# Reading the keys' columns in six orders in the products that find the score maxima

## The chip, the cores and the metric

The kernel runs on one core of one Trainium2 chip. The metric is the device time of one execution in microseconds (us). Before the change it is 1575.32 us, the median of two runs (1575.31 and 1575.34).

## The reference

Attention with 32 heads that share one head of keys and values, a gated feed-forward block (GLU), and a gate that mixes the two. All tensors are float32; S is 2048, D is 512, a head is 16 wide, F is 1792.

```python
q = (x @ wq).reshape(B, S, H, Dh).transpose(0, 2, 1, 3)
k, v = x @ wk, x @ wv                                   # one head for all
p = softmax(einsum("bhqd,bkd->bhqk", q, k) * Dh ** -0.5)
a = einsum("bhqk,bkd->bhqd", p, v) ... @ wo
b = (sigmoid(x @ w_gate) * (x @ w_up)) @ w_down
g = sigmoid((x * gate_w).sum(-1, keepdims=True))
return g * a + (1 - g) * b
```

## The kernel before, in words

The kernel makes the softmax in two passes. A **unit** is a block of 512 queries and a group of four heads; there are 32 units (4 blocks by 8 groups). For each unit the first pass makes all scores with queries on the partitions and keys along the columns, and takes the maximum of each row (`maximum`, 64 products and 64 reductions a unit, 2048 in all). The second pass makes the scores again, the other way round (`scores`, keys on the partitions), with the maximum subtracted inside the product, and ScalarE takes the exponential. The third step multiplies the exponentials with the values (`pv`).

The keys stand in SBUF in one tile `ks`, 128 partitions by 2048 columns of float32. Rows 0 to 63 and rows 64 to 127 hold copies, so that two products of 64 rows each can run beside each other on the two halves of TensorE's array. `HALF[h]` picks the half. In `maximum`, the weights (first operand) are 128 queries of one head, `qs_t[u % 3][r, pr, part(qt)]`, and the moving operand is 512 neighbouring columns of `ks`; the result is a whole PSUM bank of 128x512, from which VectorE's `tensor_reduce` takes one maximum per partition. The operands of these products, of `scores` and of the feed-forward products (`fill`) are of the type float32r; the profile prints them as f32. Of the large groups only `pv` has operands of plain float32: each of its products stands in the trace as two matmuls, 4096 for 2048, in groups of four that use four bands of 32 columns of the array together.

What runs when is fixed in the program. A long string `ORDER` names the steps, and `State.step` turns each character into instructions; nothing is decided at run time but waits on semaphores. A hex digit is one **slot**: one product for the upper half and one for the lower, decoded by `divmod(int(code, 16), 4)`, where 1 is a maximum, 2 a score and 3 a feed-forward product. So `5` is a slot with a maximum in both halves, `7` and `d` one with a maximum and a feed-forward product, `6` and `9` one with a maximum and a score. `V` is one step of `pv`, which uses the whole array. TensorE takes its products in this order; the lists of VectorE, ScalarE, GpSimd and the DMA queue follow from it. The eight banks of PSUM are shared by all.

Of the kernel before, what the change touches and what calls it, by code (L numbers as in the profile page):

```python
# [725 lines left out]
def tile_kernel(ctx, tc, x_in, wq, wkv, wo, wg, wu, wd, consts_in, out):  # L726
    nc = tc.nc
# [13 lines left out]
    banks = [pp.tile([P, 512], F32, tag=f"bank{i}", name=f"bank{i}") for i in range(8)]  # L741
# [13 lines left out]
    def split(raw, hl, hi, lo):  # L755
        hi(hl[:, 0, :], raw)
        lo.tensor_tensor(hl[:, 1, :], raw, f32(hl[:, 0, :]), op=ALU.subtract)  # L757
        return hl
# [81 lines left out]
    part = lambda i: slice(i * P, (i + 1) * P)  # L840
# [30 lines left out]
    qs_t = [cp.tile([P, 2, TB], F32R, name=f"qs{i}") for i in range(3)]  # L871
# [22 lines left out]
    ks = cp.tile([P, S], F32R, name="ks")  # L894
# [238 lines left out]
    def h_split(_, b, f):  # L1133
        hl = fp.tile([P, 2, TB], F32R, tag="hl", name=f"hl{b}_{f}", bufs=HB)
        HS[b, f] = split(HS[b, f], hl, nc.gpsimd.tensor_copy, nc.gpsimd)

    def maximum(h, n, i):
        s, pr = divmod(n, 2)
        u, n = divmod(s, NC)
        qt, kb = divmod(n, 4) if u else (n % 4, n // 4)  # L1140
        r = HALF[h]
        nc.tensor.matmul(banks[i], qs_t[u % 3][r, pr, part(qt)], ks[r, kb * 512:(kb + 1) * 512],  # L1142
                         start=True, stop=True)
        nc.vector.tensor_reduce(MX[u][:, pr, h, qt, kb:kb + 1], banks[i], axis=AX.X, op=ALU.max)  # L1144

    def scores(h, n, i):
# [13 lines left out]
        "load": load_item, "w_hi": w_hi, "w": w_split, "x_hi": x_hi, "x": x_lo,  # L1160
        "f": fill, "gate": gate, "gated": gated, "h": h_split, "part": part_of, "add": add_part, "out": send_out,
        "m": maximum, "max_finish": max_finish, "max_split": max_split, "max_square": max_square,
        "send_max": send_max, "place_max": place_max, "s": scores,
        "values": on_bank(pv), "finish": on_bank(finish), "store": store, "sums": sums, "invert": invert, "send_inverse": send_inverse,
# [28 lines left out]
    for i in range(2):  # L1193
        for j in range(4):
            for t in (2 * i, 2 * i + 1):
                r, m = HALF[t % 2], slice(32 * j, 32 * j + 32)
# [63 lines left out]
```

## Time and profile before

| | |
|---|---|
| time, two runs | 1575.34 and 1575.31 us |
| span of the profiled execution | 1573.0 us; the 2.3 us between it and the runs' times lie outside the first and last instruction |
| TensorE (PE) busy | 1564.3 us, 99% of the span, 12910 matmuls |
| VectorE (DVE) busy | 1339.4 us, 85%; the maxima's reductions alone 1254.3 us |
| ScalarE (ACT) busy | 1232.0 us, 78% |
| GpSimd (POOL) busy | 803.0 us, 51% |
| granted TensorE clock | 9 tenths or more in all 40 slices |

PE is the matmul stream, PEld the loading of weights, which overlaps it. A matmul's record covers the time from its start until its last result is there, so two records on the same half overlap; the distance from start to start tells how long a product holds its half. A group's row gives busy time and mean length of one instruction, then the idle time of the engine just before it and what ended that idle time.

### The profile page before, as it was taken

To read this page: it belongs to the slowest core of one execution; us is meant where nothing else is said; L and a number is where in the kernel's file an instruction comes from. 1 tells how busy PE (TensorE), PEld (TensorE's weight loads), DVE (VectorE), ACT (ScalarE), POOL (GpSimd) and SP (SyncE) were. 2 spreads that over 40 slices of the span, in tenths; PEclk is the share of its full clock that TensorE was granted. 3 is DMA by queue.
4 is the path that set the end of the run, shared out by engine and by line. 5 is a ranking of instruction groups with operands and counts; after the bars stand their busy time and mean duration, and the time that the engine had idled before them with its cause. 6 is when DMAs were issued, how large, how long until landed. Compare 5 with 4: busy or idle time off the path is not lost.

```text
span 1573.0 us, 33645 instructions
## 1 busy us (share of the span) xinstructions
PE 1564.3 (99%) x12910; PEld 1008.8 (64%) x12910; DVE 1339.4 (85%) x2278; ACT 1232.0 (78%) x2429; POOL 803.0 (51%) x727
## 2 busy tenths in 40 slices
PE   9999999999999999999999999999999999999998
PEld 7776766666656666666666665666665656666653
DVE  7899899988899788889798888898889888888852
ACT  4277878888788787878788787877878878787897
POOL 4253472655574164377475346265658426538351
PEclk9999999999999999999999999999999999999999
DMA  7421120212122121122121212022212212111011
GB/s 255 167 82 51 35 86 16 66 57 87 42 85 61 43 80 53 34 72 62 61 80 54 76 36 86 17 67 67 76 36 87 66 44 80 53 36 56 19 53 48
DMA packets 63220, 103.43 MB, mean 66 GB/s; under 512 B 24546, under 2 KB 25058, under 8 KB 63060
## 3 DMA queue, kind: packets, MB, share of 16 engines
q1 hardware_dynamic: 63060, 101.29, 20.3%
q8 instruction: 101, 1.65, 0.4%
q14 instruction: 59, 0.48, 0.1%
HBM read 79.51 MB, written 21.75 MB: 64 GB/s over the span
## 4 chain that ended last, share of the span: by engine, by line
PE 98%; DVE 1%; DMA 0%; issue 0%; ACT 0%; POOL 0%; SPq 0%; DVEq 0%; POOLq 0%; ACTq 0%
PE bank L1116 32%; PE bank L1009 30%; PE bank L1142 17%; PE bank L1151 16%; PE bank L854 3%; DVE mx L1144 0%; DMA xf<-x_in 0%; DVE x L787 0%; DVE ba L1207 0%; PE bank L926 0%; PE bank L1197 0%; POOL wg L830 0%; DVE q L949 0%; DVEq L1256 0%; ACT x L781 0%
## 5 line engine op out<-in xcount | busy, mean ns | idle before, releaser
L1144 DVE TENSOR_REDUCE mx<-bank 128x1 f32<-128x512 f32 x2048 | 1254.3, 682 | 168.1 <-PE bank L1142 108.3
L1153 ACT ACTIVATE p<-bank 128x512 f32<-128x512 f32 x2048 | 1040.1, 664 | 4.5 <-PE bank L1151 1.4
L1151 PE MATMUL bank<-qs,ks 64*128 64x512 f32 x2048 | 722.8, 398 | 0.0
L1142 PE MATMUL bank<-ks,qs 64*128 64x512 f32 x2048 | 683.8, 405 | 0.0
L1009 PE MATMUL bank<-p,v_aug 128*32 128x512 f32 x4096 | 480.1, 597 | 0.0
L1142 PEld LDWEIGHTS bank<-ks,qs 64*128 64x128 f32 x2048 | 339.8, 184 | 137.6 <-issue 56.1
L1151 PEld LDWEIGHTS bank<-qs,ks 64*128 64x128 f32 x2048 | 359.0, 184 | 91.3 <-ACT p L1153 27.7
L1016 ACT COPY ou<-bank 128x512 f32<-128x512 f32 x205 | 125.1, 610 | 272.5 <-PE bank L1009 122.7
L1023 POOL TENSOR_TENSOR ou<-ou,ou 128x512 f32<-128x512 f32 x174 | 224.0, 1288 | 170.8 <-ACT ou L1016 168.5
L1116 PE MATMUL bank<-wd,hl 64*128 64x512 f32 x1344 | 272.6, 391 | 0.0
L1009 PEld LDWEIGHTS bank<-p,v_aug 128*32 128x32 f32 x4096 | 113.1, 109 | 248.1 <-issue 219.3
L1116 PE MATMUL bank<-x,wu 64*128 64x512 f32 x1344 | 271.0, 390 | 0.4 <-SPq L1120 0.4
L1116 PE MATMUL bank<-x,wg 64*128 64x512 f32 x1344 | 271.2, 391 | 0.0
L1116 PEld LDWEIGHTS bank<-wd,hl 64*128 64x128 f32 x1344 | 199.9, 184 | 20.6 <-issue 2.5
L1116 PEld LDWEIGHTS bank<-x,wu 64*128 64x128 f32 x1344 | 201.1, 184 | 16.4 <-issue 2.5
L1116 PEld LDWEIGHTS bank<-x,wg 64*128 64x128 f32 x1344 | 200.4, 184 | 17.4 <-issue 1.2
L1095 POOL TENSOR_TENSOR ba<-ba,pa_d 128x512 f32<-128x512 f32 x35 | 44.5, 1282 | 93.3 <-ACT pa_d L1092 93.2
L830 POOL CAST wg<-rg 128x1024 fp32r<-128x1024 f32 x27 | 28.0, 1037 | 122.3 <-PE bank L1116 62.6
L830 POOL CAST wu<-ru 128x1024 fp32r<-128x1024 f32 x27 | 28.0, 1039 | 95.1 <-PE bank L1116 82.7
L757 POOL TENSOR_TENSOR wd<-rd,wd 128x512 fp32r<-128x512 f32 x56 | 72.4, 1293 | 4.5
L757 POOL TENSOR_TENSOR hl<-h,hl 128x512 fp32r<-128x512 f32 x56 | 72.0, 1285 | 4.5
L1116 PE MATMUL bank<-wa,o 64*128 64x512 f32 x360 | 70.5, 391 | 0.0
(80 smaller groups left out, 745.5 us busy)
## 6 DMA issues: line engine op xcount, KB each, us to landing
rg<-wg SPq DMA_DIRECT2D x28, 512.0 KB
ru<-wu SPq DMA_DIRECT2D x28, 512.0 KB
rd<-wd SPq DMA_DIRECT2D x28, 512.0 KB
qs<-qd SPq DMA_DIRECT2D x192, 64.0 KB
qd<-q SPq DMA_DIRECT2D x32, 256.0 KB
od<-ou SPq DMA_DIRECT2D x31, 256.0 KB
xf<-x_in SPq DMA_DIRECT2D x16, 256.0 KB
vd<-od SPq DMA_DIRECT2D x32, 128.0 KB
```

The costliest lines, as they stand in the source:

```text
L757: lo.tensor_tensor(hl[:, 1, :], raw, f32(hl[:, 0, :]), op=ALU.subtract)
L830: nc.gpsimd.tensor_copy(WS[item][:, 0, :], raw)
L854: nc.tensor.matmul(ps, w[:, p, part(kc)], X[b, kc][:, q, :], start=i == 0, stop=i == 3 * KC - 1)
L1009: nc.tensor.matmul(ps[32 * j:32 * j + 32, :], v_aug[:, c, :], PT.pop((u, c, j)), start=start, stop=stop)
L1016: nc.scalar.copy(to, ps)
L1023: nc.gpsimd.tensor_tensor(SUMS[u], SUMS[u], PARTS_OF[u].pop(0), op=ALU.add)
L1095: nc.gpsimd.tensor_tensor(BA[b, t], BA[b, t], PA[b, t].pop(0), op=ALU.add)
L1116: ins = nc.tensor.matmul(banks[i], l, r, start=start, stop=stop)
L1142: nc.tensor.matmul(banks[i], qs_t[u % 3][r, pr, part(qt)], ks[r, kb * 512:(kb + 1) * 512], start=True, stop=True)
L1144: nc.vector.tensor_reduce(MX[u][:, pr, h, qt, kb:kb + 1], banks[i], axis=AX.X, op=ALU.max)
L1151: nc.tensor.matmul(banks[i], ks[r, part(c)], qs_t[u % 3][r, pr, :], start=True, stop=True)
L1153: nc.scalar.activation(p, banks[i], AF.Exp, scale=0.25)
```

## The change

In `maximum`, the moving operand's 512 columns are read in an order that depends on the unit: `WAYS[u % 6]`. With `a=way`, the view `"p (a b) -> p b a"` reads `way` columns that lie 512/way apart, then moves on by one column. So way 1 is the order of before; way 2 hops 256 columns back and forth (1024 bytes); way 256 reads every second column (8 bytes apart), first the even ones and then the odd ones; way 4 reads columns 128 apart (512 bytes), way 16 columns 32 apart (128 bytes). The results are written to the bank in the order they come, without gaps, and the maximum of a row does not depend on the order. In the way "halves" the product becomes two products of 256 neighbouring columns each with the same weights, into the two halves of the bank. Units 0, 6, 12, ... have way 1 (6 units), 1, 7, ... way 2 (6), 2, 8, ... way 256 (5), 3, 9, ... way 4 (5), 4, 10, ... halves (5), and 5, 11, ... way 16 (5).

```diff
+    WAYS = 1, 2, 256, 4, "halves", 16
+
     def maximum(h, n, i):
         s, pr = divmod(n, 2)
         u, n = divmod(s, NC)
         qt, kb = divmod(n, 4) if u else (n % 4, n // 4)
         r = HALF[h]
-        nc.tensor.matmul(banks[i], qs_t[u % 3][r, pr, part(qt)], ks[r, kb * 512:(kb + 1) * 512],
-                         start=True, stop=True)
+        l, k, way = qs_t[u % 3][r, pr, part(qt)], ks[r, kb * 512:(kb + 1) * 512], WAYS[u % len(WAYS)]
+        if way == "halves":
+            for a in range(2):
+                nc.tensor.matmul(banks[i][:, a * 256:(a + 1) * 256], l, k[:, a * 256:(a + 1) * 256], start=True, stop=True)
+        else:
+            nc.tensor.matmul(banks[i].rearrange("p (b a) -> p b a", a=way), l, k.rearrange("p (a b) -> p b a", a=way),
+                             start=True, stop=True)
         nc.vector.tensor_reduce(MX[u][:, pr, h, qt, kb:kb + 1], banks[i], axis=AX.X, op=ALU.max)
```

No instruction changes its place against the others. Only the way "halves" adds some. On TensorE, where unit 4 begins (its queries are in `qs_108`), the order of before reads as follows; L1142 is a maximum's product, L1151 a score's and L1116 one of the feed-forward block:

```order
1261 L1151 MATMUL bank_78<-qs_109,ks 128x512
1262 L1116 MATMUL bank_76<-x_1_125,wu_3_2192 128x512
1263 L1116 MATMUL bank_75<-x_0_124,wu_3_2192 128x512
1264 L1142 MATMUL bank_74<-ks,qs_108 128x512
1265 L1151 MATMUL bank_77<-qs_109,ks 128x512
1266 L1116 MATMUL bank_76<-x_1_125,wu_3_2192 128x512
```

The same place of the changed kernel (a maximum's product is now L1147 where it is halved, and a score's is L1158):

```order
1261 L1158 MATMUL bank_78<-qs_109,ks 128x512
1262 L1116 MATMUL bank_76<-x_1_125,wu_3_2192 128x512
1263 L1116 MATMUL bank_75<-x_0_124,wu_3_2192 128x512
1264 L1147 MATMUL bank_74<-ks,qs_108 128x256 x2
1265 L1158 MATMUL bank_77<-qs_109,ks 128x512
1266 L1116 MATMUL bank_76<-x_1_125,wu_3_2192 128x512
```

One row of 512 columns became two of 256 that stand directly behind each other, and nothing else moved. This happens 320 times; the other 1728 products of `maximum` keep their place and their length, and 1024 of them (ways 2, 4 and 16) read columns that lie 128 bytes or more apart.

## The prediction

> **What bounds the kernel now.** I read the page first, for the engine that never rests: busy shares, the slices, and the chain that ended last.
>
> ```profile
> PE 1564.3 (99%) x12910; PEld 1008.8 (64%) x12910; DVE 1339.4 (85%) x2278; ACT 1232.0 (78%) x2429; POOL 803.0 (51%) x727
> ...
> PE   9999999999999999999999999999999999999998
> ...
> PEclk9999999999999999999999999999999999999999
> ...
> PE 98%; DVE 1%; DMA 0%; issue 0%; ACT 0%; POOL 0%; SPq 0%; DVEq 0%; POOLq 0%; ACTq 0%
> PE bank L1116 32%; PE bank L1009 30%; PE bank L1142 17%; PE bank L1151 16%; PE bank L854 3%; DVE mx L1144 0%; DMA xf<-x_in 0%; DVE x L787 0%; DVE ba L1207 0%; PE bank L926 0%; PE bank L1197 0%; POOL wg L830 0%; DVE q L949 0%; DVEq L1256 0%; ACT x L781 0%
> ```
>
> TensorE is busy in every slice, its clock is granted in full, and the chain runs through it for 98% of the span; the changed line, L1142, has 17% of it. A busy matmul row need not mean that products follow each other without gaps, so I went to the costliest groups and then to the timeline.
>
> ```profile
> L1144 DVE TENSOR_REDUCE mx<-bank 128x1 f32<-128x512 f32 x2048 | 1254.3, 682 | 168.1 <-PE bank L1142 108.3
> ...
> L1142 PE MATMUL bank<-ks,qs 64*128 64x512 f32 x2048 | 683.8, 405 | 0.0
> ...
> L1023 POOL TENSOR_TENSOR ou<-ou,ou 128x512 f32<-128x512 f32 x174 | 224.0, 1288 | 170.8 <-ACT ou L1016 168.5
> ```
>
> The second largest load, VectorE's reductions, waits 108.3 us for the very products that change, so it is behind TensorE and not ahead of it. The timeline of TensorE in the middle of the span shows the pace (columns: start in us, length in us, instruction; records on one half overlap):
>
> ```profile
> 692.33 0.39 PE L1116 MATMUL bank<-x,wg 64*128 64x512 f32 x1
> 692.33 0.39 PE L1151 MATMUL bank<-qs,ks 64*128 64x512 f32 x1
> 692.56 0.39 PE L1116 MATMUL bank<-x,wg 64*128 64x512 f32 x1
> 692.56 0.39 PE L1151 MATMUL bank<-qs,ks 64*128 64x512 f32 x1
> 692.79 0.40 PE L1116 MATMUL bank<-x,wg 64*128 64x512 f32 x2
> 693.02 0.39 PE L1151 MATMUL bank<-qs,ks 64*128 64x512 f32 x1
> 693.03 0.39 PE L1116 MATMUL bank<-x,wg 64*128 64x512 f32 x1
> 693.25 0.39 PE L1142 MATMUL bank<-ks,qs 64*128 64x512 f32 x1
> ```
>
> Products start two by two, every 0.23 us (692.33, 692.56, 692.79, 693.02, 693.25): a slot of two products, one per half, takes 0.23 us, however long each record is. There is no wait between slots. What lengthens a product lengthens its slot, and TensorE has nothing in reserve to hide it. One unit's stretch (unit 4) says the same:
>
> ```profile
> core 0: us, PE busy (x) PEld busy (x) DVE busy (x) ACT busy (x) POOL busy (x), PEclk, DMA share, GB/s
> ...
> 209.90:251.30 41.40, 41.40 (x350) 25.00 (x346) 39.46 (x68) 31.25 (x62) 24.17 (x21) 1.00 0.16 50
> ```
>
> TensorE is busy for all 41.40 us, VectorE for 39.46. If TensorE slows down, VectorE gets slack; if TensorE gets faster here, VectorE allows at most 1.94 us a unit.
>
> **The change part by part.** (1) *Ways 2, 4 and 16: hops of 1024, 512 and 128 bytes.* The change adds no instruction to these and takes none away. The products are (6 + 5 + 5) units x 64 = 1024. The question is what one costs when its moving columns are not neighbours, and no product of before reads so. From below: a gain is not excluded, but VectorE's share above caps it near 2 us a unit, so 16 units give at most about 30 us, and nothing in the rows makes a contiguous read the slow one; nothing is the lower end that I use. From above I take four column times, 4 x 0.23 = 0.92 us a product, as if each read brought four neighbours of which three are thrown away; it lies between VectorE's 0.682 us for a bank of 512 columns (L1144) and GpSimd's 1.288 us for a subtraction of 512 columns (L1023), the slowest reader among the large groups. Between the ends, the nearest row is the only one in which TensorE itself takes 512 columns at another pace, the float32 passes of `pv`; their weight loads show it:
>
> ```profile
> 702.16 0.13 PEld L1009 LDWEIGHTS bank<-p,v_aug 128*32 128x32 f32 x4 [0.30 <-issue]
> 702.59 0.13 PEld L1009 LDWEIGHTS bank<-p,v_aug 128*32 128x32 f32 x4 [0.30 <-issue]
> 703.02 0.13 PEld L1009 LDWEIGHTS bank<-p,v_aug 128*32 128x32 f32 x4 [0.30 <-issue]
> ```
>
> Four run together and the next four follow 0.43 us later: half speed. Their reason is their data type, not hops, so this is a choice by nearness: **0.43 us a product, 0.20 more**.
>
> What 0.20 us is worth depends on how the halves pair. TensorE starts products in order, so a slow product in one half holds back the other half's next but one. If every slow product holds its whole slot, slots count: in the order, 91 slots have such a maximum in both halves, so 1024 - 91 = 933 slots are longer and 933 x 0.20 = 187 us is added. If slow products of the two halves covered each other perfectly, each half's own 512 would count: 512 x 0.20 = 102 us. The halves can run apart by about a slot and no more, and most slow products stand beside a fast one; I take the middle, **+144 us**.
>
> (2) *Way 256: every second column, 8 bytes apart, 320 products.* Again no row shows it. If eight-byte steps slow the read as hops do, 0.20 us for 160 products per half up to 293 slots (27 have both halves) is 32 to 59 us. I take nothing, because neighbours in steps of two are the nearest thing to the contiguous read, and keep +45 us as a case.
>
> (3) *Halves: 320 products of 512 columns become 640 of 256, each with its own weight load.* In proportion, a half takes 0.115 us and the two 0.23: nothing. The other end is the load: if the second product waited for the whole record of its load, 0.184 us, the pair would take 0.37 us, 0.14 more; for 160 to 292 slots that is 22 to 41 us. The rows at the start of a group of slots decide:
>
> ```profile
> 691.53 0.49 PE L1116 MATMUL bank<-x,wg 64*128 64x512 f32 x1
> ...
> 691.53 0.18 PEld L1116 LDWEIGHTS bank<-x,wg 64*128 64x128 f32 x1 [0.84 <-POOL hl L757]
> ...
> 691.63 0.19 PEld L1116 LDWEIGHTS bank<-x,wg 64*128 64x128 f32 x1
> ```
>
> This product starts together with its load and lasts 0.49 us where others last 0.39: the load holds it for 0.10 us, not 0.18. The next load begins 0.10 us later, when the product streams. So a load of 0.10 fits under a half of 0.115. I take 0.02 us a product for the closer sequence: 160 to 292 times 0.02 is 3 to 6, **+5 us**. The other half's products behind the first slip by half a slot, which lies inside the distance that the halves may have.
>
> (4) *Everything else.* The reduction reads a full bank as before. Semaphores, banks and DMAs are those of before; what is queued behind the products on TensorE starts later, and all waiters with it.
>
> **Sum:** 1573.0 (span) + 144 + 0 + 5 = 1722, and 2.3 us outside the span make **1724 us**, against 1575.3 in the runs shown.
>
> The notes bear on this, and they do not agree among themselves. The Trainium skill, "Advanced Engine Details and Errata", SBUF Cachelines, says that SBUF has lines of 16 bytes and that a reader needs at least two hits on a line to run at full performance. By that rule ways 1, 256 (two float32 per line) and halves are free and ways 2, 4 and 16 pay; the page gives no price. The Trainium skill, "Vector Engine (DVE) Microarchitecture Reference", 5.2 Measured stream behaviour on trn2, has VectorE at 1.73 ns a column when one source hops at each element; if TensorE's read paid that, an estimate would be 0.886 us a product and, by the same middle of both counts, about 2054 us. Against it stands the Trainium skill, "TensorE: Matmul & The Clock Gate", Step-by-step, by which a product takes as many cycles as it has columns, with no word on their order: that is rival A. No run here shows any of the three yet.
>
> **The rivals.** *A, the order costs nothing.* If the array's feed reads a column per step from anywhere, the 1024 products stay at 0.23 us and only the halves' 5 us is left: **1580 us**, not slower by what a measurement can tell. For it: the slots keep 0.23 us whether the moving operand is `ks`, `qs` or an activation tile in quite different places, so nothing in the rows shows TensorE near a limit of its reads. It decides as soon as a hop costs under about 0.04 us a product (0.04 x 723, the middle of 512 and 933, is 29 us). *B, four column times.* 0.69 us more for 512 to 933 products is 353 to 644, in the middle 498; way 256 would then read two of four, half speed, +45; with the halves' 5 it is **2123 us**. For it: the other engines' 0.68 and 1.29 us for 512 columns show that this is no strange pace for a reader; against it: they read contiguously at that pace, so it says little of hops. *C, the forecast with way 256 slow as well*: 1724 + 45 = **1769 us**. *D, two streams are free*: way 2 alternates between just two places, and if each has its own line held, only ways 4 and 16 pay: 640 products, 56 slots with both, 320 to 584 times 0.20 is 64 to 117, middle 90: **1670 us**. *E, the order is undone when the program is built*: the built program's rows for these products have the same sizes as before and tell no order, so it can't be excluded; it gives 1580 us like A.
>
> **How the numbers follow.** The forecast has 0.30; C 0.08; D 0.07; A and E together 0.25; B 0.25; and 0.05 is for prices between A and D, the dear halves, and the small gain. The range reaches from 1577 to 2140: it leaves out the upper half of B (which spreads from about 1930 to 2290 with the pairing) and the lower part of A. The forecast's own range, by the pairing alone, is 1682 to 1767. A measurement of this kernel can tell about 2% from no change, 1544 to 1607 us. Slower than that: forecast, B, C, D and most of the rest, 0.74; within: A and E, 0.24; faster: 0.02.
>
> **What would show it.** Each unit has its own stretch of some 45 us, so one table by stretches separates the ways, and the starts in the timeline give the slot. Right: TensorE's slots near 0.43 us in units 1, 3 and 5, at 0.23 in units 0 and 2, and near 0.25 where products are halved; VectorE's waits for L1149 grow. Wrong: slots of 0.23 everywhere (A), 0.9 (B), 0.43 in unit 2 (C), 0.23 in unit 1 but 0.43 in unit 3 (D), or halves that take 0.37. The forecast fails by its size if a hop's price depends on its length, since I gave one price to 128, 512 and 1024 bytes.

## The result and the profile after

The changed kernel takes **1653.49 us** (median of two runs) against 1575.32 us before: ratio 1.0494, 95% interval 1.0464 to 1.0525. The forecast was 1724, with a range of 1577 to 2140. The direction held and the size was about half: 78 us more where 149 were expected. The spans differ by 1651.6 - 1573.0 = 78.6 us.

The page shows the same picture as before, stretched. L1149 is now the maximum's product, L1147 its halves, L1151 the reduction and L1158 the score's product:

```profile
PE 1643.1 (99%) x13230; PEld 1091.5 (66%) x13230; DVE 1362.0 (82%) x2278; ACT 1260.7 (76%) x2429; POOL 803.9 (49%) x727
...
PE 98%; DVE 1%; POOL 0%; issue 0%; DMA 0%; ACT 0%; DVEq 0%; POOLq 0%; ACTq 0%
...
L1151 DVE TENSOR_REDUCE mx<-bank 128x1 f32<-128x512 f32 x2048 | 1276.4, 683 | 222.9 <-PE bank L1149 115.8
...
L1149 PE MATMUL bank<-ks,qs 64*128 64x512 f32 x1728 | 681.8, 488 | 0.1
```

TensorE still has 98% of the chain and VectorE's idle time before its reductions grew from 168.1 to 222.9 us, so TensorE's products got slower and nothing else took over. The mean record of a maximum's product went from 405 to 488 ns, but a mean over six orders says nothing. The stretches of the units tell the orders apart. Table by stretches of the changed kernel, units 1 to 5 (ways 2, 256, 4, halves, 16), each from its first product to the first of the next unit; the second column is the length:

```profile
76.20:120.60 44.40, 44.40 (x352) 31.89 (x353) 41.25 (x69) 31.23 (x63) 20.45 (x18) 1.00 0.27 91
120.60:169.60 49.00, 49.00 (x360) 33.15 (x358) 40.23 (x66) 33.33 (x62) 16.03 (x14) 1.00 0.14 43
169.60:219.10 49.50, 49.50 (x409) 35.02 (x407) 43.48 (x74) 38.06 (x75) 25.09 (x24) 1.00 0.22 64
219.10:260.90 41.80, 41.80 (x416) 28.23 (x414) 39.71 (x68) 31.35 (x63) 23.75 (x21) 1.00 0.16 48
260.90:311.40 50.50, 50.50 (x372) 35.59 (x370) 42.92 (x69) 38.61 (x72) 16.40 (x15) 1.00 0.10 31
```

The same stretches of the kernel before:

```profile
75.70:120.30 44.60, 44.60 (x352) 32.12 (x353) 41.31 (x69) 31.23 (x63) 20.43 (x18) 1.00 0.26 91
120.30:162.30 42.00, 42.00 (x360) 28.23 (x356) 38.17 (x66) 30.79 (x62) 16.02 (x14) 1.00 0.17 50
162.30:209.90 47.60, 47.60 (x408) 32.30 (x406) 42.88 (x74) 37.58 (x76) 24.65 (x23) 1.00 0.22 66
209.90:251.60 41.70, 41.70 (x350) 25.27 (x348) 39.71 (x68) 31.39 (x63) 24.17 (x21) 1.00 0.16 50
251.60:295.30 43.70, 43.70 (x370) 28.41 (x368) 40.63 (x69) 35.76 (x72) 16.37 (x15) 1.00 0.12 34
```

Five readings: way 2, the longest hop, is 0.2 us *shorter*; way 256, steps of 8 bytes, is 7.0 us longer; way 4 is 1.9 longer; the halves cost 0.1; way 16 is 6.8 longer. All 32 units behave like these. Summed over the units of each way (unit starts taken to the nanosecond from the records), the changes are +0.8 us (way 1), -1.4 (way 2), +37.0 (way 256), +8.2 (way 4), +0.5 (halves) and +33.6 (way 16), 78.7 in all.

The records of the products themselves, in the same five units (min, median and max length in ns; way 2, way 256, way 4, halves, way 16):

```profile
L1149 PE MATMUL bank<-ks,qs x64: 373/375/480, 76.2 to 119.6; 64*128 64x512 f32 x64
L1149 PE MATMUL bank<-ks,qs x61: 607/622/712, 120.6 to 169.2; 64*128 64x512 f32 x61
L1149 PE MATMUL bank<-ks,qs x68: 428/434/630, 169.2 to 218.1; 64*128 64x512 f32 x68
L1147 PE MATMUL bank<-ks,qs x128: 271/278/384, 219.1 to 260.8; 64*128 64x256 f32 x128
L1149 PE MATMUL bank<-ks,qs x63: 589/591/681, 260.9 to 310.5; 64*128 64x512 f32 x63
```

Before, the median was 392. A record is longer than the time for which its product holds its half, so I also took, from the records and the order in `ORDER`, the distance from the start of a maximum's product to the next start on its half; below this is called the **pace**. Medians over all units of a way: 233 ns contiguous, 215 way 2, 437 way 256, 273 way 4, 417 way 16, and 118 for each half of 256. So a record is 160 to 185 ns longer than the pace (392 against 233 for the contiguous order), and the two sort the orders alike.

### The profile page after: what moved, and what is told of

It is laid out like the page before. It is cut to its first block, busy times and chain, and to the rows that moved or that the text cites. A ratio compares the mean times of both kernels' runs of the same rounds, so it can differ in the third digit from the quotient of the medians.

```text
span 1651.6 us, 34485 instructions
## 1 busy us (share of the span) xinstructions
PE 1643.1 (99%) x13230; PEld 1091.5 (66%) x13230; DVE 1362.0 (82%) x2278; ACT 1260.7 (76%) x2429; POOL 803.9 (49%) x727
## 4 chain that ended last, share of the span: by engine, by line
PE 98%; DVE 1%; POOL 0%; issue 0%; DMA 0%; ACT 0%; DVEq 0%; POOLq 0%; ACTq 0%
PE bank L1116 30%; PE bank L1009 28%; PE bank L1149 19%; PE bank L1158 16%; PE bank L854 3%; PE bank L1147 2%; DVE mx L1151 0%; DMA wkv_raw<-wkv 0%; POOL wkv_s L757 0%; DVE ba L1214 0%; PE bank L926 0%; PE bank L1204 0%; POOL wg L830 0%; DVE wkv_stack L890 0%; DVE q L949 0%
## 5 line engine op out<-in xcount | busy, mean ns | idle before, releaser
L1151 DVE TENSOR_REDUCE mx<-bank 128x1 f32<-128x512 f32 x2048 | 1276.4, 683 | 222.9 <-PE bank L1149 115.8
L1160 ACT ACTIVATE p<-bank 128x512 f32<-128x512 f32 x2048 | 1061.2, 639 | 28.0 <-PE bank L1158 7.5
L1158 PE MATMUL bank<-qs,ks 64*128 64x512 f32 x2048 | 725.2, 400 | 0.0
L1149 PE MATMUL bank<-ks,qs 64*128 64x512 f32 x1728 | 681.8, 488 | 0.1
L1158 PEld LDWEIGHTS bank<-qs,ks 64*128 64x128 f32 x2048 | 361.8, 185 | 77.6 <-issue 23.9
L1149 PEld LDWEIGHTS bank<-ks,qs 64*128 64x128 f32 x1728 | 288.8, 186 | 112.0 <-issue 58.9
L1116 PE MATMUL bank<-wd,hl 64*128 64x512 f32 x1344 | 286.2, 392 | 0.0
L1116 PE MATMUL bank<-x,wg 64*128 64x512 f32 x1344 | 281.8, 392 | 0.0
L1116 PE MATMUL bank<-x,wu 64*128 64x512 f32 x1344 | 281.3, 391 | 0.0
L1116 PEld LDWEIGHTS bank<-wd,hl 64*128 64x128 f32 x1344 | 209.4, 185 | 17.8 <-issue 3.2
L1116 PEld LDWEIGHTS bank<-x,wu 64*128 64x128 f32 x1344 | 210.0, 185 | 14.4 <-issue 2.1
L1116 PEld LDWEIGHTS bank<-x,wg 64*128 64x128 f32 x1344 | 206.6, 185 | 17.1 <-issue 2.2
L1147 PEld LDWEIGHTS bank<-ks,qs 64*128 64x128 f32 x640 | 96.0, 185 | 21.8 <-issue 7.5
L1147 PE MATMUL bank<-ks,qs 64*128 64x256 f32 x640 | 108.4, 283 | 0.0
```

The costliest lines, as they stand in the source:

```text
L1116: ins = nc.tensor.matmul(banks[i], l, r, start=start, stop=stop)
L1147: nc.tensor.matmul(banks[i][:, a * 256:(a + 1) * 256], l, k[:, a * 256:(a + 1) * 256], start=True, stop=True)
L1149: nc.tensor.matmul(banks[i].rearrange("p (b a) -> p b a", a=way), l, k.rearrange("p (a b) -> p b a", a=way), start=True, stop=True)
L1158: nc.tensor.matmul(banks[i], ks[r, part(c)], qs_t[u % 3][r, pr, :], start=True, stop=True)
L1160: nc.scalar.activation(p, banks[i], AF.Exp, scale=0.25)
```

## The experiments

**Which orders are slow (e1).** The 512 columns in sixteen further orders, and two orders of writing the bank:

```diff
+    WAYS = ("S8", "S32", "S64", "S128", "D128", "D64", "D32", "D16", "D8", "D4", "D2", "Q2", "Q16", "Q128", "out", "both")
+    # S: "p (a b) -> p b a", a=n;  D: "p (o t b) -> p o b t", t=2, b=n;  Q: "p (a b c) -> p b a c", a=n, c=2
```

> Sixteen ways of reading the 512 columns, one per unit (unit u has way u % 16, so two units each). S: n single columns, 512/n apart, in turn. D: two columns in turn, n columns apart. Q: n neighbouring pairs of columns in turn. out: contiguous read, written to the bank in pairs 256 columns apart. both: read and written so. What is read off is the distance from a maximum's product to the next product on its half; in the changed kernel it was 227 to 236 ns for the contiguous read, 215 for two columns 1024 bytes apart, 271 for four 512 bytes apart, 416 for sixteen 128 bytes apart, 437 for steps of 8 bytes. Theory 1, the distance decides (two columns are fetched in one step, free if they lie in one pair of neighbours or in different banks, and a long distance is another bank): D128 (512 bytes) about 240 to 270, D64 (256 bytes) about 300 to 350, D32 to D2 416 to 437; S8 (256 bytes) 300 to 400, S32, S64 and S128 416 to 437; pairs Q2, Q16, Q128 at 215 to 237. Theory 2, the number of streams decides (some lines are held): every D way 215 whatever its distance, S8 and above about 416 or more, Q2 215, Q16 and Q128 slower. Writes: 227 to 236 in the way out if the order in the bank costs nothing, up to about 430 if it does. The whole kernel about 1620 to 1690 us.

The kernel took 1683.47 us in one run. The product's records in one unit each of S8, S128, D128, D4, D2, Q2, out and both (the product is L1167 here):

```profile
L1167 PE MATMUL bank<-ks,qs x64: 663/712/791, 818.7 to 875.6; 64*128 64x512 f32 x64
L1167 PE MATMUL bank<-ks,qs x64: 615/619/702, 982.3 to 1032.1; 64*128 64x512 f32 x64
L1167 PE MATMUL bank<-ks,qs x64: 373/375/481, 1037.1 to 1081.2; 64*128 64x512 f32 x64
L1167 PE MATMUL bank<-ks,qs x65: 373/376/480, 1269.8 to 1313.9; 64*128 64x512 f32 x65
L1167 PE MATMUL bank<-ks,qs x64: 385/390/497, 1316.7 to 1359.9; 64*128 64x512 f32 x64
L1167 PE MATMUL bank<-ks,qs x63: 483/492/596, 1360.8 to 1412.9; 64*128 64x512 f32 x63
L1167 PE MATMUL bank<-ks,qs x64: 383/392/501, 1523.8 to 1570.0; 64*128 64x512 f32 x64
L1167 PE MATMUL bank<-ks,qs x63: 485/497/589, 1572.8 to 1623.9; 64*128 64x512 f32 x63
```

The distance theory fell: two columns in turn are equally fast at 512 bytes (375) and at 16 bytes (376), and only at 8 bytes (D2) like the contiguous read. But "two streams are free" does not explain Q2, also two streams, which is slow (492), nor why the contiguous read, one stream, is slower than two. Writing the bank in pairs of columns that lie 1024 bytes apart costs nothing: 392 for out, as contiguous, and 497 for both against 492 for Q2, which reads alike.

**Two readers? (e6).** What sorts these results is to deal the columns by turns to two readers and count how many of its columns each finds one after another in 16 bytes (four columns). Contiguous: 0, 2 and then the next line, two. Way 2 and D4 to D128: 0, 1, 2, 3, four. Way 256, S128, Q16 and Q128: one. Two streams with a step of their own test it, since the streams stay and the count falls:

```diff
+    # T: "p (t o s) -> p s o t", t=2, s=n;  S: "p (a b) -> p b a", a=n;  V: "p (t g o) -> p o g t", t=2, g=n;  C: unchanged
+    WAYS = ("T1", "T2", "T4", "T8", "T16", "S4", "V2", "C1")
```

> Eight ways, four units each. T: two columns 256 apart in turn, and along each of the two streams a step of n columns (T1 is the way 2 of the changed kernel). S4: four columns 128 apart in turn. V2: the same four places, in the order 0, 256, 128, 384. C1: contiguous. Theory (columns go by turns to two readers, and each wants several of its columns from one 16-byte line one after another): T1 gives each reader four per line, 215 ns; T2 two per line, 227 to 236 like the contiguous read, which also gives each reader two; T4, T8 and T16 one per line, 410 to 440. Rival (it is the two streams as such that are fast, whatever their step): T2, T4, T8, T16 all 215. S4 about 271 as measured; V2 the same if only the number of lines per reader counts, less or more if their distance does.

1675.07 us in one run. Records of T1, T2, T4, T16, S4 and V2 in one unit each (L1165 here):

```profile
L1165 PE MATMUL bank<-ks,qs x64: 373/375/480, 417.1 to 462.4; 64*128 64x512 f32 x64
L1165 PE MATMUL bank<-ks,qs x64: 384/392/502, 463.1 to 506.4; 64*128 64x512 f32 x64
L1165 PE MATMUL bank<-ks,qs x64: 609/626/712, 509.1 to 559.2; 64*128 64x512 f32 x64
L1165 PE MATMUL bank<-ks,qs x65: 586/592/685, 615.6 to 667.9; 64*128 64x512 f32 x65
L1165 PE MATMUL bank<-ks,qs x64: 428/433/538, 669.0 to 717.2; 64*128 64x512 f32 x64
L1165 PE MATMUL bank<-ks,qs x63: 428/433/538, 718.6 to 766.5; 64*128 64x512 f32 x63
```

All eight came out as the theory says, T2 like the contiguous read (T8 has 620, C1 392), and the rival, that two streams are fast whatever their step, is out. The paces of both surveys and of the changed kernel together:

| a reader's columns per 16 bytes | orders | pace, median ns |
|---|---|---|
| four in a row | way 2 = T1, D128, D64, D32, D16, D8, D4 | 215 to 216 |
| two in a row | contiguous, D2, T2 | 231 to 233 |
| one | way 256, T4, T8, S128, Q16, Q128 | 434 to 443 |
| one | S64, S32, way 16, T16 | 413 to 419 |
| two lines by turns, one column each time | way 4 = S4, V2; Q2 | 273; 327 |
| four lines by turns, one column each time | S8 | about 530 |

The Trainium skill's rule ("Advanced Engine Details and Errata", SBUF Cachelines: at least two hits on a line) read for the whole stream had way 2 slow and way 256 free, and both came out the other way. Read for every second column it parts the first two rows (215 to 233 ns) from the next two (413 to 443), but not the first from the second. That there really are two readers is inferred from the counts, and no run shows them otherwise. What the counts leave open is why the two rows with one column differ, why Q2 is dearer than way 4, and why four lines by turns cost more than one column of each.

**Do the halves keep step? (e2).** The slow way 16 in one half alone, in both, or in every other product:

```diff
+    def slow(u, h, n):
+        return (False, h == 0, h == 1, True, (h + n) % 2 == 0, False)[u % 6]
```

> Sixteen columns in turn, 128 bytes apart (the way that takes 0.416 us instead of 0.23), used in part of the products: units with u % 6 = 1 in the upper half alone, 2 in the lower half alone, 3 in both, 4 in every other product of each half, 0 and 5 nowhere. Theory (each half keeps its own pace and they drift apart): a unit gets longer by its own half's 32 x 0.187 = 6.0 us, the same for upper, lower and both, and by 3.0 for every other product. Rival (slots are kept in step, starts in program order): both 58 slots x 0.187 = 10.8 us, or between 6 and 10.8, against 6.0 for one half, and every other product about 6.

1697.72 us in one run. Stretches of units 7 to 10 (upper, lower, both, every other):

```profile
366.20:421.90 55.70, 55.70 (x422) 35.33 (x420) 45.04 (x74) 44.43 (x82) 31.95 (x26) 1.00 0.22 66
421.90:473.80 51.90, 51.90 (x394) 34.72 (x393) 42.66 (x70) 38.52 (x73) 26.54 (x24) 1.00 0.15 48
473.80:527.30 53.50, 53.50 (x381) 30.36 (x377) 43.46 (x72) 42.22 (x80) 33.40 (x31) 1.00 0.21 64
527.30:578.60 51.30, 51.30 (x410) 35.07 (x406) 41.35 (x69) 37.78 (x73) 16.16 (x16) 1.00 0.20 60
```

The same stretches of the kernel before:

```profile
341.30:391.20 49.90, 49.90 (x424) 30.40 (x422) 43.32 (x75) 42.10 (x83) 31.91 (x26) 1.00 0.24 74
391.20:437.30 46.10, 46.10 (x395) 31.04 (x392) 40.55 (x70) 36.60 (x74) 26.55 (x24) 1.00 0.14 44
437.30:483.20 45.90, 45.90 (x379) 25.82 (x376) 41.78 (x72) 39.08 (x79) 32.84 (x29) 1.00 0.26 85
483.20:530.90 47.70, 47.70 (x412) 30.93 (x408) 40.34 (x69) 36.88 (x73) 16.80 (x19) 1.00 0.22 66
```

Over all units of a kind, the upper half alone adds 5.9 us, the lower 5.8, both 7.4, every other product 3.6. One half's price is 6.0 = 32 x 0.187; doubling the slow products adds only a quarter more. So slow products of the two halves mostly cover each other, and the lock-step count of 10.8 is far off. The changed kernel's trace shows how. In program order, product 675 is a feed-forward one and 676 a score's:

```
675 L1116 MATMUL bank_72<-x_0_124,wg_2_1195 128x512
676 L1158 MATMUL bank_78<-qs_107,ks 128x512
```

Its timeline has them the other way round, behind two slow maxima on the two halves:

```profile
130.84 0.84 PE L1149 MATMUL bank<-ks,qs 64*128 64x512 f32 x2
131.36 0.41 PE L1158 MATMUL bank<-qs,ks 64*128 64x512 f32 x1
131.50 0.41 PE L1116 MATMUL bank<-x,wg 64*128 64x512 f32 x1
```

Here a half that was free took its next product before the other half's earlier one had started. By the records, the two products of a slot start up to 1.2 us apart in the units of e2 with one slow half, some five slots.

**The fast order for all maxima (e3).**

```diff
-        nc.tensor.matmul(banks[i], qs_t[u % 3][r, pr, part(qt)], ks[r, kb * 512:(kb + 1) * 512],
+        nc.tensor.matmul(banks[i].rearrange("p (b a) -> p b a", a=2), qs_t[u % 3][r, pr, part(qt)],
+                         ks[r, kb * 512:(kb + 1) * 512].rearrange("p (a b) -> p b a", a=2), start=True, stop=True)
```

> Two columns in turn, 1024 bytes apart, in all 2048 maxima. If the 0.215 us slot of that way is worth what units 1, 7, ... showed (0.23 us less per unit), 32 units give 7.4 us: 1568 us, ratio 0.995. If the whole 0.015 us of each of a half's 1024 products counts, 15 us: 1560. If VectorE's reductions hold the pace, or unit 1's gain was chance: 1575.

1570.63 us, ratio 0.9965 (0.9953 to 0.9978): 5.6 us less than the kernel before in the same series (1576.21), a gain of a third of a percent, near the first expectation (7.4) and a third of what the shorter pace would give by itself (15).

**The fast order for every product of 64 rows (e4, e5).** Scores and feed-forward products read their moving operand in the same way; where ScalarE and VectorE empty a bank, they read it back in the right order:

```diff
-        nc.scalar.copy(to, ps)
+        nc.scalar.copy(plain(to), back(ps))      # back: "p (b a) -> p a b", plain: "p (a b) -> p a b", a=2
-        nc.tensor.matmul(banks[i], ks[r, part(c)], qs_t[u % 3][r, pr, :], start=True, stop=True)
+        nc.tensor.matmul(came(banks[i]), ks[r, part(c)], two(qs_t[u % 3][r, pr, :]), start=True, stop=True)
-        ins = nc.tensor.matmul(banks[i], l, r, start=start, stop=stop)
+        ins = nc.tensor.matmul(came(banks[i]), l, two(r), start=start, stop=stop)
```

(`two` and `came` are the two views of e3; gate, product and parts of the feed-forward block read with `back` too.)

> All products of 64 rows (maxima, scores, feed-forward, output) read two columns 256 apart in turn; the results are put straight again where ScalarE and VectorE read the banks (205 + 56 + 56 + 84 instructions with steps of 8 bytes in PSUM); the exponentials stay in the turned order up to the copy of the sums. A slot takes 215 instead of about 231 ns if both its products read so: about 4250 slots x 0.016 = 66 us if nothing else holds: 1510 us, ratio 0.958. Rival, VectorE: its 1339 us are 95% of the densest units, and the order of work was laid out for the longer slot, so that TensorE then waits for banks: a gain of 20 to 45 us, 1530 to 1555. Second rival: the stepped reads of the banks cost as much as the products save: 1575.

> The same for the 4404 feed-forward and output products alone; maxima and scores read contiguously. If each half's own products count, 2202 x 0.016 = 35 us less, 1540; if only slots with two such products get shorter, 869 slots x 0.016 = 14 us less, 1561; if the stepped reads of the banks cost more than that, 1575 or above.

> The same for the 2048 maxima and 2048 scores alone; the feed-forward products read contiguously. If each half's own products count, 2048 x 0.016 = 33 us less, 1543; if only slots with two such products get shorter, 192 + 225 + 223 + 74 = 714 slots x 0.016 = 11 us less, 1564; the maxima alone gave 5.6 us less than the kernel before.

All: 1564.54 us, ratio **0.9925** (0.9910 to 0.9940), the fastest version that computes the whole reference. Feed-forward alone: 1572.97 us, 0.9981 (0.9971 to 0.9990). Maxima and scores: 1568.03 us, 0.9947 (0.9930 to 0.9964). Against 1576.39 us for the kernel before in the same series, these are 11.9, 3.4 and 8.4 us less. The 3.4 is less than either count of the feed-forward products gave (35 and 14); the 8.4 lies near the lower count of maxima and scores (11). In e4 the median pace of all three kinds is 216 ns, as hoped, and yet 12 of the expected 66 us arrived, fewer than the 20 to 45 of the rival too. The waits of the kernel before, of TensorE's weight loads for banks that ScalarE's exponentials hold (us in total, times, longest):

```profile
PEld bank L1142 <- ACT p L1153: 31.1, 59, 0.8
...
PEld bank L1151 <- ACT p L1153: 27.7, 69, 0.8
```

and of e4, the same two groups:

```profile
PEld bank L1163 <- ACT p L1165: 51.6, 188, 0.8
PEld bank L1154 <- ACT p L1165: 43.1, 122, 0.8
```

128 waits became 310. To test whether these waits take the gain, the next four leave work out: e7 half of every exponential (the values' products read the first 256 columns twice), e8 also half of every maximum's columns, each with the contiguous order and with that of e4.

```diff
-        nc.scalar.activation(p, banks[i], AF.Exp, scale=0.25)
+        nc.scalar.activation(p[:, :256], banks[i][:, :256], AF.Exp, scale=0.25)
-        nc.vector.tensor_reduce(MX[u][:, pr, h, qt, kb:kb + 1], banks[i], axis=AX.X, op=ALU.max)
+        nc.vector.tensor_reduce(MX[u][:, pr, h, qt, kb:kb + 1], banks[i][:, :256], axis=AX.X, op=ALU.max)
```

> The kernel before, but each exponential covers 256 of the 512 columns, and the values' products read these 256 twice: half of ScalarE's main work is left out, TensorE's is the same. If TensorE alone sets the time, 1570 to 1575 us. It is the base for the next run.

> All 64-row products read two columns in turn, with the same half of the exponentials left out. If ScalarE's banks took back most of the 66 us that the shorter slots were worth, the difference to the run before this one rises from 12 to 40 to 60 us: 1510 to 1535. If VectorE's reductions took it, the difference stays near 12 and comes with the next pair. If the shorter slots are lost inside TensorE itself, neither pair shows it.

> The kernel before with half of the exponentials and the second half of each maximum's columns left out (the reduction reads 256 of 512 columns). Base for the next run; 1565 to 1575 us if TensorE alone sets the time.

> The same left out, all 64-row products reading two columns in turn. If the waits for the banks of ScalarE and VectorE together took the gain, the difference to the run before this one is 55 to 66 us: about 1505 to 1515. If it is 12 again, the loss is inside TensorE: the halves' products do not start as soon as their columns allow.

The last two rows are of another series than the first, in which the kernel before took 1577.20 us; the ratios are to that.

| left out | contiguous, us | two columns in turn, us | difference |
|---|---|---|---|
| nothing | 1576.39 | 1564.54 | 11.9 |
| half the exponentials | 1566.93 (0.9934, 0.9920 to 0.9949) | 1546.02 (0.9800, 0.9785 to 0.9814) | 20.9 |
| and half the maxima's columns | 1558.80 (0.9883, 0.9868 to 0.9897) | 1508.97 (0.9565, 0.9549 to 0.9581) | 49.8 |

With half of the exponentials left out and the order of e4 (e7), the waits for ScalarE fall and those for VectorE's reductions take their place:

```profile
PEld bank L1163 <- DVE mx L1156: 33.2, 143, 0.8
PEld bank L1154 <- DVE mx L1156: 16.8, 59, 0.8
PEld bank L1154 <- ACT p L1165: 15.9, 19, 0.8
PEld bank L1163 <- ACT p L1165: 10.9, 13, 0.8
```

In e4 the first two were 8.8 and 9.2 us. So the loss lies in the waits for both engines, and not inside TensorE: ScalarE alone gave back less than expected (21, not 40 to 60), both together 50 us. That is under the expected 55 to 66, but these counted on 231 ns for the contiguous order; in the relieved kernel (e8) its median pace is 227 ns against 216, and 4250 slots times 11 ns are 47 us. Nothing of the gain is missing there. Why the contiguous pace itself falls from 231 to 227 when the other engines do less stays open, and so does whether an order of work laid out for slots of 0.215 us would keep the gain without leaving anything out.

The two contiguous kernels came out below what was expected of them if TensorE alone sets the time (1570 to 1575 and 1565 to 1575). So TensorE alone does not quite set the time of the kernel before: it gets 10 us shorter with half of the exponentials left out and 18 us with half of the maxima's columns left out too; the 4 ns of pace in 4250 slots are 17 of these.

## Why the prediction was right in direction and half in size

- **What bounds the kernel** held for this change: TensorE's slots carried it, and no other engine took over. "No wait between slots" holds for the stretch shown and not throughout: its weight loads waited 58.8 us for banks that the exponentials held, and by e8 some 18 us of its time go when ScalarE and VectorE have half of their work.
- **Step 1, the price of a hop** (0.20 us, one price for ways 2, 4 and 16) is the step that failed. The size was right for way 16 alone (+0.184 from the medians 417 and 233). Way 4 cost 0.040 and way 2 gained 0.018. The mistake was to give every hop one price; what sorts the prices, by e1 and e6, is how many of every second column follow each other in one 16 bytes. The last sentence of the prediction named this risk, though by the length of a hop, which e1 shows not to matter for two columns by turns from 16 to 1024 bytes. Forecast for the three ways +144 us, measured -1.4 + 8.2 + 33.6 = +40.4.
- **The pairing** (the middle between 512 and 933 products) was too dear as well. By e2 one half's 32 products add 5.8 to 5.9 us and those of both halves 7.4, a quarter above one half's count; the middle was 41% above it. The sentences behind it are wrong: across the halves products do not always start in order, and the halves ran apart by up to 1.2 us in e2, not by a slot of 0.23.
- **Step 2, way 256 at nothing**, failed in the other direction: 0.437 us a product and +37.0 us. The case kept beside it (+45) had the price of a product right, 0.20 us. With it the sum would have been rival C's 1769 us, better founded and yet farther from the time: **the sum is half right because two wrong steps partly cancel**, 104 us too much in step 1 and 37 too little in step 2. That the sum came as near as it did is luck.
- **Step 3, the halves** held: 5 us forecast, 0.5 measured. Each half's pace is 118 ns, half of the contiguous product's, so the load of the weights is hidden, as its 0.10 us of hold suggested, and the second product costs nothing that the trace shows.
- **Step 4** held: VectorE's waits for the maxima's products grew from 108.3 to 115.8 us, and no other engine came into the chain.
- **The rivals.** D's 1670 us came nearest to the time, nearer than the forecast, but by the same luck: it had ways 4 and 16 at 90 us (measured 41.8) and way 256 at nothing (37.0). Its thought, that two streams are free, was right for way 2 and is not the reason (Q2, T4). Rival A was right for way 2 alone, and C's price for way 256 was right.

## What to carry to other kernels

For the float32r products of this kernel, whose moving operand lies contiguous, reading two streams by turns (columns 0, 4, 1, 5 and so on, or 0, 256, 1, 257) shortens the pace from about 231 to 215 ns per 512 columns. It costs nothing where the order of the results doesn't matter. Where ScalarE or VectorE puts the order right as it empties the bank, the stepped read cost nothing either: ScalarE's gate took 598 ns against 599 and VectorE's product 677 against 677 (e7, all products turned and none). Do not read such an operand in one stream with steps of two or four columns: 8 bytes (437 ns) and 16 bytes (441) are as dear as hops of 128, nearly twice the time.

And a shorter pace of the bounding engine shortens the time only as far as the engines that empty its banks keep up. Here it was worth up to 66 us of 1575 by the count of slots, and 12 arrived until both of them had less to do.

## What the runs showed of the hardware that was not expected

- The contiguous read is not the fastest: 233 ns against 215 for two streams at 16 to 1024 bytes, and 227 against 216 with ScalarE and VectorE relieved (e8). Half the columns take half of it (118 ns for 256).
- Steps of 8 bytes (437 ns) cost more than hops of 128 bytes (417), and two columns by turns, 1024 bytes apart, cost less than neighbours (215 against 233).
- The order in which a bank is written, in pairs 1024 bytes apart, costs nothing (392 ns contiguous, 392 so written).
- Products in the two halves of the array can start out of the program's order (131.36 us for product 676, 131.50 for 675).
